# Moving side work between the steps of a fused FNet and gated-FFN kernel

## The chip, the cores and the metric

The kernel runs on one core of one Trainium2 chip. A core has five engines that run side by side, each through its own list of instructions in order: TensorE (PE, matmuls; PEld is its weight load), VectorE (DVE), ScalarE (ACT), GpSimd (POOL) and SyncE (SP, which here only issues DMAs). They wait for each other through semaphores. The metric is the device time of one execution in microseconds, from the first to the last instruction; less is better.

## The reference

The input x has shape (8, 3008, 256), all in float32. A Fourier transform along the sequence and one along the features is taken, and the real part kept. The 8 x 3008 = 24064 rows then pass through a gated feed-forward block.

```python
def _attn_ref(x):
    X = np.fft.fft(x, axis=1)
    X = np.fft.fft(X, axis=2)
    return X.real.astype(np.float32)

def _moe_ref(x, w_gate, w_val, w_out):      # (24064,256) (256,1536) (256,1536) (1536,256)
    gate = 1.0 / (1.0 + np.exp(-(x @ w_gate)))
    val = x @ w_val
    return (gate * val @ w_out).astype(np.float32)
```

## The kernel before

The kernel uses the symmetry of the transform. For a batch, x is loaded as `x4` (128 partitions, 4 mirrored quarters, 6, 256), and *folds* on GpSimd add and subtract the quarters and the mirrored features in place. The sequence transform is then four groups of matmuls (`ev`, `od`) of the folded x with a table `st` of cosines and sines. Each group is *evacuated*: ScalarE copies `ev` out of PSUM, and two sums on VectorE write it into a tile `pk` or `qk` (a third one, `ek`, comes for batches 1 to 7 from `x8`, one feature column of all of x, through `e_fold` and `e_sums`). The feature transform is merged into the weights once, at the start (`G1`, `G2`).

The body is a loop of steps. A batch has 6 chunks of up to 256 columns and 6 pairs of hidden blocks for each, 2 steps a pair: 12 steps a chunk, 72 a batch, 576 in all. While a batch is computed, the next one is folded and transformed in the side jobs of these steps.

```python
def front(p, fh):                    # step: the two matmul pairs, then VectorE
    ...
    for g in range(2):
        mm(pa[:, g], G1[:, g, fs], pk[:, ks], g == 0, True)
    for g in range(2):
        mm(pb[:, g], G2[:, g, fs], qk[:, ks], g == 0, True)
    ae = app.tile(...)
    for g in range(2):
        nc.vector.scalar_tensor_tensor(out=ae[:, g], in0=ek[:, ks], scalar=ge[:, g, f : f + 1],
                                       in1=pa[:, g], op0=ALU.mult, op1=ALU.add)
    z = zp.tile(...)
    nc.vector.tensor_tensor(z[:, :, 0], ae, pb, op=ALU.add)
    nc.vector.tensor_tensor(z[:, :, 1, ::-1], ae, pb, op=ALU.subtract)

def gate(p, fh, z):                  # one step later; h holds the products, sf sums of them
    ...
    nc.vector.tensor_tensor(h[:, fh], z[:, 0], z[:, 1], op=ALU.mult)
    if fh == 0:
        tt(s[:, 2], h[:, 0, 0], h[:, 0, 1], op=ALU.subtract)      # tt is on GpSimd
    else:
        tt(s[:, 0], h[:, 0, 1], h[:, 1, 1], op=ALU.add)
        tt(s[:, 1], s[:, 0], h[:, 0, 0], op=ALU.subtract)
        tt(s[:, 3], h[:, 1, 0], s[:, 1], op=ALU.subtract)

def back(p, part):                   # two pairs later: 3 or 4 products of h or sf with wf, into po
    ...
    if part == 0 and i == NPR - 1:   # copies of po by ScalarE; after the last part: finish
        ...

def finish(b, c, last):              # after a chunk: one job a step from `later`
    ...
    for j in (0, 2, 1):
        nc.scalar.copy(t[:, 2 * j : 2 * j + 2, 0:n], PO[j][:, :, 0:n])
    later.extend([
        lambda: tt(v[:, 0:2], v[:, 6:7].to_broadcast([P, 2, n]), v[:, 0:2], op=ALU.add),
        ...                          # five adds on GpSimd (tile c), then
        lambda: flip(0, 0, 0),       # four transposes on VectorE, and the stores of the output
        ...

fresh = None
for i in range(2 * len(pairs)):
    done, fresh = fresh, front(i // 2, i % 2)
    if done is not None:
        gate(*done)
    if i >= 4:
        back(i // 2 - 2, i % 2)
    ...
    nc.scalar.activation(z[:, 0], z[:, 0], AF.Sigmoid)
    if later:
        later.pop(0)()
    for f in side.pop(i, []):        # side jobs: folds, groups of the transform, loads
        f()
```

A chunk ends in step 3 of the next one, so its five adds fall in steps 3 to 7 of a chunk and its transposes in steps 8 to 11. `side` is filled with `at(i, job)`; `split(i, f)` puts the matmuls and ScalarE's copy in step i and VectorE's sums in step i + 1:

```python
i0 = 2 * NPR                         # 12
at(i0 + 1, e_load, lambda: load_x(1))
for b in range(B - 1):
    s0 = b * per                     # 72 b
    if b:
        at(s0 + 1, lambda b=b: load_x(b + 1))
        if b < B - 2:
            at(s0 + 20, lambda b=b: mirror_x(b + 2))
    f0, g0, gs = (s0 + 9, s0 + 36, 8) if b else (i0 + 9, i0 + 36, 7)
    def folds(f0=f0, b=b):
        for j, f in enumerate(fold_ops(b + 1, 2)):     # 24 jobs
            at(f0 + j, f)
    at(f0 - 1, folds)
    at(g0 - 3, lambda b=b: seq_start(b + 1))
    for j in range(4):
        split(g0 + gs * j, whole, b + 1, j // 2, j % 2)
at(i0 + 14, e_fold)
split(i0 + 18, e_sums)
at(i0 + 20, table_again)
at(8, lambda: mirror_x(1))
at(i0 + 3, mirror_tables, lambda: mirror_x(2))
```

`mirror_x(b)` makes a copy of x in DRAM (`xr`) with the mirrored rows in order, by 9 DMAs; `mirror_tables` does the same for the table (`tr`), which `table_again` loads in place of the first one. All of these are issued by SyncE, as are the stores of the output.

Of the kernel before, what the change touches and what calls it, by code (L numbers as in the profile page):

```python
# [44 lines left out]
NQ = 6  # L45
NP = 126
HP = 64
# [4 lines left out]
def kernel(  # L52
# [10 lines left out]
    nc = tc.nc  # L63
    B, _, _, _, D = xf.shape
# [3 lines left out]
    M = S // 2  # L68
    NK = M + 1
    NE = (M // 2) // 2 + 1  # L70
    NO = (M // 2) // 2
# [4 lines left out]
    HD = D // 2  # L76
    TB = 32
    N3 = NQ // 2
# [31 lines left out]
    def load_x(b):  # L110
        X[b] = xp.tile([P, 4, NQ, D], F32, name="x4", tag="x4")
        for h in range(0, 4, 2):
            if b:
                nc.sync.dma_start(out=X[b][:, h : h + 2], in_=XR[b][:, h : h + 2])
            else:
                nc.sync.dma_start(out=X[b][0:NP, h : h + 2], in_=xf[b, :, h : h + 2])

    def mirrored(dst, src, full):

        for par in range(2):  # L120
            lo = par * HP
            nc.sync.dma_start(out=dst[lo : lo + HP, :, 0:N3], in_=src[0:HP, :, par:NQ:2])
            for q in range(N3):
                t = M // 2 - 2 * q - par
                p0, n = t // NQ, HP - 2 * ((par, q) == (0, N3 - 1))
                nc.sync.dma_start(
                    out=dst[lo : lo + n, :, N3 + q, full:].rearrange("p h d -> h p d"),
                    in_=src[p0 - n + 1 : p0 + 1, :, t % NQ, full:].rearrange("p h d -> h p d")[:, ::-1])

    XR = {}  # L130

    def mirror_x(b):
        XR[b] = dram.tile([P, 4, NQ, D], F32, name=f"xr{b}")
        mirrored(XR[b], xf[b], 0)

        nc.sync.dma_start(out=XR[b][HP - 2 : HP, :, NQ - 1],
                          in_=zero[:, :, 0:D].to_broadcast([2, 4, D]))

    dt = const.tile([P, 2, D], F32, name="dt")
    ST = [const.tile([P, 2, NQ, NE + NO], F32, name="st", tag="st")]  # L140
# [5 lines left out]
    x8 = const.tile([NP, B - 1, 4, NQ], F32, name="x8")  # L146
    zero = const.tile([2, 1, NO], F32, name="zero")
    tr = dram.tile([P, 2, NQ, NE + NO], F32, name="tr")
# [4 lines left out]
            nc.sync.dma_start(out=ST[0][0:NP, t, q : q + nq], in_=stab[:, t, q : q + nq])  # L153

    def mirror_tables():
        mirrored(tr, stab, NE)
        nc.sync.dma_start(out=tr[HP - 2 : HP, :, NQ - 1, NE:],
                          in_=zero.to_broadcast([2, 2, NO]))

    def table_again():  # L160

# [72 lines left out]
    def weight_use(j, other=None):  # L234
        w, c = jobs[j]
        if w == 2:
            forms(WS.pop(j), c)
        else:
            merge(WS.pop(j), w, c, other)
# [14 lines left out]
    def forms(ws, c):  # L254

        w = ws.rearrange("p f (a h j) -> p f h a j", h=2, j=TB)
        f = wf[:, c].rearrange("p m (a j) -> p m a j", j=TB)
        sub = lambda o, a, b: nc.gpsimd.tensor_tensor(o, a, b, op=ALU.subtract)
        nc.scalar.copy(f[:, 0:2], w[:, :, 0])
        nc.scalar.copy(f[:, 2], w[:, 1, 1])  # L260
        sub(f[:, 4], w[:, 0, 1], w[:, 0, 0])
        sub(f[:, 6], w[:, 1, 1], w[:, 0, 1])
        sub(f[:, 5], w[:, 1, 1], f[:, 4])
        sub(f[:, 3], w[:, 1, 0], f[:, 5])
# [4 lines left out]
    def fold_ops(b, nq):  # L269
        x4 = X.pop(b)  # L270
        if not b:
            x4 = x4[0:NP]
        ops = []

        def point(e, i, j, q):
            e.tensor_tensor(x4[:, i, q, 1:D], x4[:, i, q, 1:D], x4[:, j, q, D - 1 : 0 : -1],
                            op=ALU.add)

        def first(e, i, j, q):
            e.tensor_tensor(x4[:, i, q, 0], x4[:, i, q, 0], x4[:, j, q, 0], op=ALU.add)  # L280

        def feat(e, v, r, q):
            e.memset(r[:, q, 0:1], 0.0)
            e.tensor_tensor(r[:, q, 1:HD], v[:, q, 1:HD], v[:, q, D - 1 : HD : -1],  # L284
                            op=ALU.subtract)
            e.tensor_tensor(v[:, q, 1:HD], v[:, q, 1:HD], v[:, q, D - 1 : HD : -1], op=ALU.add)  # L286

        def across(e, blk, q):
            e.tensor_tensor(x4[:, 1 - blk, q], x4[:, 0, q], x4[:, 2, q],  # L289
                            op=(ALU.add, ALU.subtract)[blk])  # L290

        parts = [(x4[:, 1], x4[:, 3]), (x4[:, 0], x4[:, 2])]
        qs = [slice(q, q + nq) for q in range(0, NQ, nq)]
        pool = nc.gpsimd
        if b:

            for i in (0, 2):
                ops += [lambda i=i, q=q: point(pool, i, i + 1, q) for q in qs]
                ops.append(lambda i=i: first(pool, i, i + 1, slice(0, NQ)))
            for blk in range(2):  # L300
                ops += [lambda blk=blk, q=q: across(pool, blk, q) for q in qs]
            for i, op in enumerate((ALU.add, ALU.subtract)):
                for ds in (slice(0, HD), slice(HD, D)):
                    ops.append(lambda i=i, op=op, ds=ds: pool.tensor_tensor(
                        x4[:, 3, i * N3 : (i + 1) * N3, ds], x4[:, 1, 0:N3, ds],
                        x4[:, 1, N3:, ds], op=op))
            parts[0] = x4[:, 3], x4[:, 1]
            for v, r in parts:
                ops += [lambda v=v, r=r, q=q: feat(pool, v, r, q) for q in qs]
        else:  # L310

            def half1(q):
                point(nc.vector, 2, 3, q)
                first(nc.vector, 2, 3, q)
                for blk in range(2):
                    across(nc.vector, blk, q)
                    feat(nc.vector, *parts[blk], q)

            def half2(q):
                across(nc.vector, 0, q)  # L320
                feat(nc.vector, *parts[0], q)
                across(pool, 1, q)
                feat(pool, *parts[1], q)
            for q in qs:
                point(nc.vector, 0, 1, q)
            first(nc.vector, 0, 1, slice(0, NQ))
            point(pool, 2, 3, qs[1])
            first(pool, 2, 3, qs[1])
            ops += [lambda: half1(qs[0]), lambda: half2(qs[1])]
        for blk, (v, r) in enumerate(parts):  # L330
            W[b, blk] = (v[:, :, 0:HD], r[:, :, 0:HD],
                         v[:, :, HD : HD + 1].to_broadcast([v.shape[0], NQ, P]))
        return ops
# [43 lines left out]
    def seq_start(b):  # L377
        PQE[b] = (pqp.tile([P, NK], F32, name="pk", tag="pk"),
                  pqp.tile([P, NK], F32, name="qk", tag="qk"),
                  pqp.tile([P, NK], F32, name="ek", tag="ek"))  # L380
        if b:
            nc.sync.dma_start(out=PQE[b][2], in_=ed[b - 1 : b, :].to_broadcast([P, NK]))
# [2 lines left out]
        return half(lambda q: W[b, blk][what][:, q, :], PQE[b][what], blk, what == 1, other)  # L385


    def e_load():
        for b in range(1, B):
            nc.sync.dma_start(out=x8[:, b - 1], in_=xf[b, :, :, :, HD : HD + 1])  # L390

    def e_fold():
        tt = nc.gpsimd.tensor_tensor
# [32 lines left out]
    pairs = [(b, c, i) for b in range(B) for c in range(len(chunks)) for i in range(NPR)]  # L426
# [162 lines left out]
    for i, f in enumerate(fold_ops(0, NQ // 2)):  # L589
        f()  # L590
        for sums, _, _ in cos:
            sums(*range(i * NQ // 2, (i + 1) * NQ // 2))
# [14 lines left out]
    def at(i, *fs):  # L607
        side.setdefault(i, []).extend(fs)

    def split(i, f, *args):  # L610

        at(i, lambda: at(i + 1, f(*args)))
# [9 lines left out]
    for j in range(3, len(jobs)):  # L622
        w, c = jobs[j]
        at(2 * c + (-3, -2, 1)[w], lambda j=j: weight_use(j))
    i0 = 2 * NPR
    at(i0 + 1, e_load, lambda: load_x(1))

    for b in range(B - 1):
        s0 = b * per
        if b:  # L630
            at(s0 + 1, lambda b=b: load_x(b + 1))
            if b < B - 2:
                at(s0 + 20, lambda b=b: mirror_x(b + 2))
        f0, g0, gs = (s0 + 9, s0 + 36, 8) if b else (i0 + 9, i0 + 36, 7)

        def folds(f0=f0, b=b):
            for j, f in enumerate(fold_ops(b + 1, 2)):
                at(f0 + j, f)
        at(f0 - 1, folds)
        at(g0 - 3, lambda b=b: seq_start(b + 1))  # L640
        for j in range(4):
            split(g0 + gs * j, whole, b + 1, j // 2, j % 2)
    at(i0 + 14, e_fold)
    split(i0 + 18, e_sums)
    at(i0 + 20, table_again)
    at(8, lambda: mirror_x(1))
    at(i0 + 3, mirror_tables, lambda: mirror_x(2))

    fresh = None
    for i in range(2 * len(pairs)):  # L650
# [71 lines left out]
```

## Time and profile before

| | |
|---|---|
| median of 3 runs | 2024.16 us (2021.05 to 2027.18) |
| profiled execution, span | 2017.1 us |
| granted TensorE clock, mean | 0.997 |
| folds of x on GpSimd, 24 jobs a batch (batches 1 to 7) | 1.44 us (points), 1.36 us (across), 1.03 us, 0.93 + 0.86 us (features) for one instruction |
| adds after a chunk on GpSimd (tile c) | 1.56, 1.31, 0.98, 0.72, 0.72 us |
| sums of `h` on GpSimd (tile sf), 4 a pair | 0.74 to 0.77 us each |
| evacuation of a group | 0.47 us on ScalarE, 2 x 0.54 us on VectorE |
| all DMA traffic | 100.32 MB, mean 50 GB/s |

In a row of the profile L100 is the line of the matmul helper, so groups are told apart by their tiles: `po<-sf` is a matmul that reads `sf` and writes `po`. A fp32 matmul shows as two instructions. Behind an arrow in brackets stands how long an engine sat idle before an instruction, and what released it. In a table of waits the columns are the total in us, the number of waits, and the longest.

### The profile page before, as it was taken

To read this page: it belongs to the slowest core of one execution; us is meant where nothing else is said; L and a number is where in the kernel's file an instruction comes from. 1 tells how busy PE (TensorE), PEld (TensorE's weight loads), DVE (VectorE), ACT (ScalarE), POOL (GpSimd) and SP (SyncE) were. 2 spreads that over 40 slices of the span, in tenths; PEclk is the share of its full clock that TensorE was granted. 3 is DMA by queue.
4 is the path that set the end of the run, shared out by engine and by line. 5 is a ranking of instruction groups with operands and counts; after the bars stand their busy time and mean duration, and the time that the engine had idled before them with its cause. 6 is when DMAs were issued, how large, how long until landed. Compare 5 with 4: busy or idle time off the path is not lost.

```text
span 2017.1 us, 28127 instructions
## 1 busy us (share of the span) xinstructions
PE 1977.4 (98%) x9504; PEld 1729.7 (86%) x9504; DVE 1753.4 (87%) x3221; ACT 499.1 (25%) x876; POOL 1361.6 (68%) x1704
## 2 busy tenths in 40 slices
PE   6999999999999999999999999999999999999998
PEld 4888788888988889888898888988889888898888
DVE  7999888988899888998889987998879987898887
ACT  3422222222222222222222222222222222222221
POOL 3778755985569755796558954689546885555655
PEclk9999999999999999999999999999999999999999
DMA  7363302200022001210022100221002010000001
GB/s 274 90 141 114 103 11 78 93 12 11 16 96 70 11 12 37 103 43 14 17 75 72 32 17 11 74 75 35 12 11 74 19 28 12 11 16 16 11 16 25
DMA packets 160814, 100.32 MB, mean 50 GB/s; under 512 B 128419, under 2 KB 151715, under 8 KB 157994
## 3 DMA queue, kind: packets, MB, share of 16 engines
q1 hardware_dynamic: 158850, 98.00, 16.6%
q8 instruction: 76, 1.25, 0.3%
q10 hardware_dynamic: 1822, 0.54, 0.1%
q14 instruction: 66, 0.54, 0.1%
HBM read 73.74 MB, written 50.17 MB: 61 GB/s over the span
## 4 chain that ended last, share of the span: by engine, by line
PE 68%; POOL 20%; DVE 8%; DMA 2%; issue 2%; ACT 0%; DVEq 0%; POOLq 0%; SPq 0%; ACTq 0%
PE po L100 29%; PE pa L100 17%; PE pb L100 16%; PE ev L100 4%; POOL sf L464 3%; POOL sf L461 2%; POOL sf L463 2%; POOL x L289 2%; POOL sf L465 2%; DVE h L459 2%; DVE ae L444 2%; POOL x L286 2%; DVE z L448 1%; POOL x L284 1%; DVE z L447 1%
## 5 line engine op out<-in xcount | busy, mean ns | idle before, releaser
L659 ACT ACTIVATE z<-z 128x512 f32<-128x512 f32 (+1 forms) x576 | 358.5, 622 | 1274.8 <-DVE z L448 1274.7
L444 DVE SCALAR_TENSOR_TENSOR ae<-ek,ge,pa 128x256 f32<-128x256 f32 (+1 forms) x1152 | 490.0, 466 | 182.3 <-PE pa L100 177.9
L100 PE MATMUL pb<-qk,G 128*128 128x256 f32 (+1 forms) x2304 | 582.2, 375 | 3.3 <-DVE ae L444 2.5
L100 PE MATMUL pa<-pk,G 128*128 128x256 f32 (+1 forms) x2304 | 584.6, 376 | 0.0
L100 PE MATMUL po<-sf,wf 128*128 128x256 f32 (+1 forms) x2304 | 537.8, 376 | 12.5 <-POOL sf L464 11.2
L100 PEld LDWEIGHTS po<-sf,wf 128*128 128x128 f32 x2304 | 435.9, 190 | 68.7 <-POOL sf L464 14.4
L100 PEld LDWEIGHTS pa<-pk,G 128*128 128x128 f32 x2304 | 435.2, 190 | 60.2 <-issue 11.3
L100 PEld LDWEIGHTS pb<-qk,G 128*128 128x128 f32 x2304 | 436.9, 190 | 55.8 <-DVE ae L444 4.0
L463 POOL TENSOR_TENSOR sf<-h 128x256 f32<-128x256 f32 (+1 forms) x288 | 213.7, 742 | 364.7 <-DVE h L459 364.7
L459 DVE TENSOR_TENSOR h<-z 128x512 f32<-128x512 f32 (+1 forms) x576 | 447.7, 777 | 0.0
L447 DVE TENSOR_TENSOR z<-ae,pb 128x512 f32<-128x512 f32 (+1 forms) x576 | 390.1, 677 | 61.7 <-DVE ae L444 2.3
L100 PE MATMUL po<-h,wf 128*128 128x256 f32 (+1 forms) x1728 | 412.5, 375 | 0.0
L448 DVE TENSOR_TENSOR z<-ae,pb 128x512 f32<-128x512 f32 (+1 forms) x576 | 386.3, 671 | 0.0
L100 PEld LDWEIGHTS po<-h,wf 128*128 128x128 f32 x1728 | 328.3, 190 | 37.1
L461 POOL TENSOR_TENSOR sf<-h 128x256 f32<-128x256 f32 (+1 forms) x288 | 222.1, 771 | 190.5 <-DVE h L459 185.7
L464 POOL TENSOR_TENSOR sf<-sf,h 128x256 f32<-128x256 f32 (+1 forms) x288 | 215.2, 747 | 22.6
L465 POOL TENSOR_TENSOR sf<-h,sf 128x256 f32<-128x256 f32 (+1 forms) x288 | 214.3, 744 | 22.6
L100 PE MATMUL ev<-st,x 63*128 63x376 f32 (+4 forms) x372 | 103.5, 421 | 7.6 <-DVE x L286 6.9
L100 PE MATMUL od<-st,x 63*128 63x376 f32 (+4 forms) x372 | 102.4, 418 | 0.0
L100 PEld LDWEIGHTS ev<-st,x 63*128 63x128 f32 (+1 forms) x372 | 65.1, 188 | 39.7 <-issue 10.4
L546 ACT COPY c<-po 128x512 f32<-128x512 f32 (+1 forms) x141 | 76.8, 581 | 63.1 <-PE po L100 63.1
L506 DVE STREAM_TRANSPOSE os<-c 128x256 f32<-128x256 f32 x192 | 83.9, 437 | 0.2
(91 smaller groups left out, 806.9 us busy)
## 6 DMA issues: line engine op xcount, KB each, us to landing
x<-xr SPq DMA_DIRECT2D x14, 1536.0 KB
out_dram<-os SPq DMA_DIRECT2D x288, 64.0 KB
xr<-in_xf_dram SPq DMA_DIRECT2D x14, 768.0 KB
xr<-in_xf_dram SPq DMA_DIRECT2D x35, 256.0 KB
ek<-ed SPq DMA_DIRECT2D x7, 752.5 KB
out_dram<-os SPq DMA_DIRECT2D x92, 56.0 KB
x<-in_xf_dram SPq DMA_DIRECT2D x2, 1512.0 KB
tr<-in_stab_dram SPq DMA_DIRECT2D x2, 1129.5 KB
```

The costliest lines, as they stand in the source:

```text
L100: nc.tensor.matmul(o, l, r, start=start, stop=stop, skip_group_check=True)
L444: nc.vector.scalar_tensor_tensor(out=ae[:, g], in0=ek[:, ks], scalar=ge[:, g, f : f + 1], in1=pa[:, g], op0=ALU.mult, op1=ALU.add)
L447: nc.vector.tensor_tensor(z[:, :, 0], ae, pb, op=ALU.add)
L448: nc.vector.tensor_tensor(z[:, :, 1, ::-1], ae, pb, op=ALU.subtract)
L459: nc.vector.tensor_tensor(h[:, fh], z[:, 0], z[:, 1], op=ALU.mult)
L461: tt(s[:, 2], h[:, 0, 0], h[:, 0, 1], op=ALU.subtract)
L463: tt(s[:, 0], h[:, 0, 1], h[:, 1, 1], op=ALU.add)
L464: tt(s[:, 1], s[:, 0], h[:, 0, 0], op=ALU.subtract)
L465: tt(s[:, 3], h[:, 1, 0], s[:, 1], op=ALU.subtract)
L506: nc.vector.transpose(os_[:, s, 0:nb, h, :], t[:, slot, 0 : nb * TB])
L546: nc.scalar.copy(t[:, 2 * j : 2 * j + 2, 0:n], PO[j][:, :, 0:n])
L659: nc.scalar.activation(z[:, 0], z[:, 0], AF.Sigmoid)
```

## The change

Each chunk of 12 steps is divided: steps 3 to 7, in which GpSimd has the five adds of the chunk before, are kept free of folds (`quiet` yields the other seven), and the groups of the transform stand in step 3 (for the first batch in steps 3 and 6). Two smaller parts: x is loaded 6 steps earlier (from step 72 b + 1 to 72 b - 5), and the DMAs that copy from DRAM to DRAM become a list of which one is put in each step (`calm` yields steps 3 to 7). As folds now come earlier or later than before, the feature folds of the part that only the last two groups needed are done first, and those groups come first.

```diff
@@ fold_ops, batches 1 to 7
             for blk in range(2):
                 ops += [lambda blk=blk, q=q: across(pool, blk, q) for q in qs]
+            ops += [lambda q=q: feat(pool, *parts[1], q) for q in qs]
             for i, op in enumerate((ALU.add, ALU.subtract)):
                 ...
             parts[0] = x4[:, 3], x4[:, 1]
-            for v, r in parts:
-                ops += [lambda v=v, r=r, q=q: feat(pool, v, r, q) for q in qs]
+            ops += [lambda q=q: feat(pool, *parts[0], q) for q in qs]
@@ the copies in DRAM: `mirrored` returns 9 single jobs (the zero row first) instead of issuing all
@@ e_load
-    def e_load():
-        for b in range(1, B):
-            nc.sync.dma_start(out=x8[:, b - 1], in_=xf[b, :, :, :, HD : HD + 1])
+    def e_load(b):
+        nc.sync.dma_start(out=x8[:, b - 1], in_=xf[b, :, :, :, HD : HD + 1])
@@ the side jobs
     i0 = 2 * NPR
-    at(i0 + 1, e_load, lambda: load_x(1))
+    quiet = lambda lo: (i for i in range(lo, 2 * len(pairs)) if not 3 <= i % i0 <= 7)
+    calm = lambda lo: (i for i in range(lo, 2 * len(pairs)) if 3 <= i % i0 <= 7)
+    for i, f in enumerate(mirror_x(1)):
+        at(i0 - 3 + i // 2, f)
+    at(i0 + 2, lambda: load_x(1))
+    for b in range(1, B):
+        at(i0 + 2 + b, lambda b=b: e_load(b))
+    for i, f in zip(range(i0 + 3, 2 * i0), mirror_tables()):
+        at(i, f)
+    at(2 * i0 + 3, e_fold)
+    split(2 * i0 + 5, e_sums)
+    at(2 * i0 + 8, table_again)
 
     for b in range(B - 1):
         s0 = b * per
         if b:
-            at(s0 + 1, lambda b=b: load_x(b + 1))
-            if b < B - 2:
-                at(s0 + 20, lambda b=b: mirror_x(b + 2))
-        f0, g0, gs = (s0 + 9, s0 + 36, 8) if b else (i0 + 9, i0 + 36, 7)
-
-        def folds(f0=f0, b=b):
-            for j, f in enumerate(fold_ops(b + 1, 2)):
-                at(f0 + j, f)
-        at(f0 - 1, folds)
-        at(g0 - 3, lambda b=b: seq_start(b + 1))
-        for j in range(4):
-            split(g0 + gs * j, whole, b + 1, j // 2, j % 2)
-    at(i0 + 14, e_fold)
-    split(i0 + 18, e_sums)
-    at(i0 + 20, table_again)
-    at(8, lambda: mirror_x(1))
-    at(i0 + 3, mirror_tables, lambda: mirror_x(2))
+            at(s0 - 5, lambda b=b: load_x(b + 1))
+
+        def folds(f0=s0 - 1 if b else i0 + 8, b=b):
+            for i, f in zip(quiet(f0), fold_ops(b + 1, 2)):
+                at(i, f)
+        at(s0 - 2 if b else i0 + 7, folds)
+        groups = [s0 + i0 * k + 3 for k in (2, 3, 4, 5)] if b else [
+            i0 * k + d for k in (4, 5) for d in (3, 6)]
+        at(groups[0] - 2, lambda b=b: seq_start(b + 1))
+        for j, g in enumerate(groups):
+            split(g, whole, b + 1, 1 - j // 2, j % 2)
+        if b < B - 2:
+            for i, f in zip(calm(s0 + 2 * i0 + 9), mirror_x(b + 2)):
+                at(i, f)
```

In a batch after the first, with steps counted from its start, the folds thus stand in step -1, 0 to 2, 8 to 14, 20 to 26 and 32 to 37 (before: 9 to 32), and the groups in steps 27, 39, 51 and 63 (before: 36, 44, 52 and 60).

More of the change, by code (lines that the diff above doesn't have):

```diff
@@ L118, in mirrored, with rows, mirror @@
     def mirrored(dst, src, full):
-        for par in range(2):
[L121 to L128, printed above, removed]
+        copy = nc.sync.dma_start
+        h, n = dst.shape[1], dst.shape[3] - full
+        ops = [lambda: copy(out=dst[HP - 2 : HP, :, NQ - 1, full:],
+                            in_=zero[:, :, 0:n].to_broadcast([2, h, n]))]
+        def rows(par):
+            copy(out=dst[par * HP : (par + 1) * HP, :, 0:N3], in_=src[0:HP, :, par:NQ:2])
+        def mirror(par, q):
+            t = M // 2 - 2 * q - par
+            lo, p0, n = par * HP, t // NQ, HP - 2 * ((par, q) == (0, N3 - 1))
+            copy(out=dst[lo : lo + n, :, N3 + q, full:].rearrange("p h d -> h p d"),
+                 in_=src[p0 - n + 1 : p0 + 1, :, t % NQ, full:].rearrange("p h d -> h p d")[:, ::-1])
+        for par in range(2):
+            ops.append(lambda par=par: rows(par))
+            ops += [lambda par=par, q=q: mirror(par, q) for q in range(N3)]
+        return ops
     XR = {}
@@ L133, in mirror_x @@
         XR[b] = dram.tile([P, 4, NQ, D], F32, name=f"xr{b}")
-        mirrored(XR[b], xf[b], 0)
-        nc.sync.dma_start(out=XR[b][HP - 2 : HP, :, NQ - 1],
-                          in_=zero[:, :, 0:D].to_broadcast([2, 4, D]))
+        return mirrored(XR[b], xf[b], 0)
     dt = const.tile([P, 2, D], F32, name="dt")
@@ L155, in mirror_tables @@
     def mirror_tables():
-        mirrored(tr, stab, NE)
-        nc.sync.dma_start(out=tr[HP - 2 : HP, :, NQ - 1, NE:],
-                          in_=zero.to_broadcast([2, 2, NO]))
+        return mirrored(tr, stab, NE)
     def table_again():
```

## The prediction

> **What bounds the kernel now.** I read the page first, then the waits of all engines, then TensorE's and GpSimd's instructions in order of time around the waits that end at TensorE. The page's engine line, and its chain of work that ended last:
>
> ```profile
> PE 1977.4 (98%) x9504; PEld 1729.7 (86%) x9504; DVE 1753.4 (87%) x3221; ACT 499.1 (25%) x876; POOL 1361.6 (68%) x1704
> PE 68%; POOL 20%; DVE 8%; DMA 2%; issue 2%; ACT 0%; DVEq 0%; POOLq 0%; SPq 0%; ACTq 0%
> ```
>
> TensorE looks full. The 20% for GpSimd in the chain are not 20% to win: the chain prefers the producer even where its result came just in time. What TensorE lost is in the waits (total us, times, longest):
>
> ```profile
> PEld po L100 <- POOL sf L464: 14.4, 8, 1.9
> PE po L100 <- POOL sf L464: 11.2, 8, 1.5
> PEld po L100 <- POOL sf L465: 6.0, 15, 1.0
> PE pb L100 <- DVE ae L444: 2.5, 3, 1.4
> ```
>
> Eight waits for `sf`, one in each of batches 1 to 6 and two in batch 0. TensorE's order of time in batch 1 shows what one costs (start, length, then what ran):
>
> ```profile
> 411.86 1.03 PE L100 MATMUL pa<-pk,G 128*128 128x256 f32 x4
> ...
> 415.31 1.03 PE L100 MATMUL pa<-pk,G 128*128 128x256 f32 x4
> ...
> 424.86 1.03 PE L100 MATMUL pa<-pk,G 128*128 128x256 f32 x4
> ...
> 428.25 2.37 PE L100 MATMUL po<-sf,wf 128*128 128x256 f32 x8 [1.50 <-POOL sf L464]
> 430.45 1.03 PE L100 MATMUL pa<-pk,G 128*128 128x256 f32 x4
> ```
>
> Each `pa` starts a step. A step with eight `po` instructions lasts 415.31 - 411.86 = 3.45 us; the one at step 35 of the batch lasts 430.45 - 424.86 = 5.59 us. So one wait costs 2.14 us, more than the 1.50 the trace calls idle, because the end of a matmul is modelled. Twelve undisturbed steps take 6 x (3.45 + 3.02) = 38.8 us, the same in every chunk of batch 7, which has no folds: the rest of the time TensorE runs at its own pace. GpSimd in the same moments:
>
> ```profile
> 420.34 1.27 POOL L551 TENSOR_TENSOR c<-c 128x512 f32<-128x512 f32 x1
> ...
> 421.61 0.72 POOL L284 TENSOR_TENSOR x<-x 128x254 f32<-128x254 f32 x1
> ...
> 422.41 1.07 POOL L286 TENSOR_TENSOR x<-x 128x254 f32<-128x254 f32 x1
> ...
> 424.13 0.72 POOL L552 TENSOR_TENSOR c<-c 128x256 f32<-128x256 f32 x1
> ...
> 425.65 1.05 POOL L286 TENSOR_TENSOR x<-x 128x254 f32<-128x254 f32 x1
> ...
> 427.47 0.72 POOL L464 TENSOR_TENSOR sf<-sf,h 128x256 f32<-128x256 f32 x1
> ```
>
> It never rests: adds of the chunk that ended (`c`), folds of the next batch (`x`) and `sf` take turns, and the `sf` that TensorE waits for ends at 428.19.
>
> [...] 98% busy, and yet steps of 5.59 beside 3.45; I use starts of `pa`, not busy time. [...] The only such VectorE instruction of a step is `h`; its mean in 40 us with folds, and in 40 us without:
>
> ```profile
> L459 DVE TENSOR_TENSOR h<-z 128x512 f32<-128x512 f32 x12 | 11.6, 966 | 0.0
> ...
> L459 DVE TENSOR_TENSOR h<-z 128x512 f32<-128x512 f32 x12 | 8.2, 685 | 0.0
> ```
>
> [...] 0.28 us a step dearer, and GpSimd operations of 0.72 us that take 1.07 to 1.18. [...] a load behind others comes late:
>
> ```profile
> 113.21 17.06 SPq L390 DMA_DIRECT2D x<-in_xf_dram  x7
> 130.88 2.20 SPq L114 DMA_DIRECT2D x<-xr  x2
> ...
> 149.54 12.37 SPq L126 DMA_DIRECT2D tr<-in_stab_dram  x3
> ```
>
> and GpSimd's first fold of batch 1 sits 4.00 us idle before 138.96, waiting for that `x`.
>
> **The change, part by part.** No instruction is added or removed; all is a matter of place.
>
> *Folds out of steps 3 to 7 of a chunk.* GpSimd's work in two steps: four `sf` of 0.73, about 0.8 apart, 3.0 us; two folds of 1.27, or feature folds of 0.1 + 0.72 + 0.72, with 0.4 for each lost turn, 2.9 to 3.8; two of the five `c` adds (1.56 + 1.31 + 0.98 + 0.72 + 0.72 = 5.3 in five steps), 2.1. Before, in steps 27 to 31: 3.0 + 3.8 + 2.1 = 8.9 us in a pair of steps of 6.47, so 2.4 us of arrears a pair, about 6 in five steps. After: 3.0 + 2.1 = 5.1 there (1.4 a pair won back), 5.9 to 6.8 elsewhere, about even. The arrears of step 35 should not build up. Removed: 5.59 - 3.45 plus a trifle of 0.05 two steps earlier, 2.19 us in each of six batches = 13.1 us. In batch 0 the steps begin at 211.54, 216.82, 219.85, 225.44: 5.28 - 3.45 = 1.83 and 5.59 - 3.45 = 2.14, together 4.0 us.
>
> *Evacuations at step 3.* A group costs TensorE the same wherever it stands: at step 36, 435.78 - 430.45 = 5.33 against 3.02, and 0.1 in the next step. VectorE's two sums of 0.54 now fall where it has no transposes (0.44 each), TensorE's 2.4 or 4.1 us of group let VectorE catch up, and ScalarE's copies of `po` are done within the group. But I see no wait of TensorE there before: 0 us won.
>
> *x sooner.* Batch 0 loses GpSimd's 4.00 us idle, but TensorE did not wait then: 0. In later batches the load goes out 6 steps earlier, the fold starts 10 earlier; about 4 steps (13 us) plus the lag of GpSimd remain, and the load took about 10 us (two slices of the DMA view after its issue at 316.4). Hidden.
>
> *Copies one a step.* SyncE does not follow the steps; it runs ahead until an instruction of its own queue waits. The copies wait for nothing but older copies, so they still go out in bunches, now two of five and four between the output's stores. 0 us. Around the table they do matter. The seven loads of `x8` used to go first; now they alternate with the copies of the table and stand behind `x`. Until the last `x8`: `x` 10.1, seven loads of 2.2 = 15.4, two row copies of 3.2 = 6.4, three mirrors of 4.2 = 12.6, sum 44.5 us [...]. From the mirrored x's landing, about 116, that is 160.5. The fold of `x8` was at 154.3 before and would be reached at about 154 to 157 now; TensorE reaches the sums of it at step 29, 155.4 + 3.45 = 158.9. With 1.1 us for the fold TensorE may wait 161.6 - 158.9 = 2.7 us, and GpSimd loses some 5. I count +3 us, once.
>
> *VectorE in batch 0.* After the sums, two operations on `er` of 1.5 and 1.6 us put VectorE back; steps 34 to 38 lose 2.1 us altogether. With folds out of steps 27 to 31, half may go: -1.
>
> *A shorter lead.* The fold of the features that group one needs ends its last slice in step 25; the group stands in step 27, the distance was 4 steps before. GpSimd's folds ran 1.5 to 3 steps behind their place in steps 9 to 25 of the profile; the matmuls of the last slice stand two thirds into the group. Nearly tight: +0.4 us in six batches, about +2.5.
>
> Sum: -13.1 - 4.0 - 1 + 3 + 2.5 = -12.6, rounded to -13 with other trifles. 2024.2 - 13 is 2011; I lean one further down, 2010, as the two risks are taken at more than their likeliest size.
>
> **The rivals.** (a) *All arrears go and no risk comes true*: -18, 2006. For it: GpSimd was the only cause of the eight large waits; even before, folds in all of steps 9 to 25 with the `c` adds in five of them caused no wait. (b) *The wait moves*: the group at step 27 waits for features, or `sf` now comes late at steps 14 or 26, some 2 us a batch as before: 2020 to 2026. Against it: slack of about three steps, and loads even with the pace. (c) *VectorE becomes the bound*: its step is 2 x 0.47 + 0.69 + 0.68 + 0.69 = 3.0, with folds 3.3, with a transpose 3.7, against 3.24; folds now share steps 8 to 11 with the transposes, four times 0.45 us of arrears. Against it: the profile had that in steps 20 to 23 too, without a wait, since four banks of `pa` and `pb` hold a step. It would make +0.5 us in some chunks, up to 2020. (d) *The table's copies stall batch 0* longer, 8 to 10 us once: 2016.
>
> **Range and chances.** The lower end is (a) with a few us of spread (single times lie between 2021 and 2027): 2001. The upper end is (d), or a good part of (b): 2019. Two per cent are 40 us; TensorE's losses found above are 13.1 + 4.0 + 2.1 = 19, so faster by 2% is all but excluded, and slower by 2% would need 3 us lost in each chunk: 0.01 and 0.02.
>
> **What would show it.** Right: waits of `po` for `sf` near 0, every step 35 at 3.45 us; groups still adding about 2.4 and 4.2 us; GpSimd's total busy time about as before, `h` too. Wrong: `ev` waiting for a fold of `x` at step 27; `pe` waiting for the fold of `x8` by more than 5 us; waits of `pb` for VectorE in most batches; or `x` landing after its first fold's turn in batches 2 to 7.

## The result and the profile after

The changed kernel takes 2009.95 us (median of 4 runs, 2009.52 to 2012.41) against 2024.94 us before: ratio 0.9931, 95% interval 0.9913 to 0.9948, 0.7% faster. Forecast: 2010.0, between 2001 and 2019. Close as that is, two terms of its sum were well off and in opposite directions, and a part of the gain was not in the sum at all.

The page of the changed kernel, its engine line and the chain that ended last:

```profile
PE 1975.4 (98%) x9504; PEld 1738.0 (87%) x9504; DVE 1767.0 (88%) x3221; ACT 498.3 (25%) x876; POOL 1332.2 (66%) x1704
PE 92%; DMA 3%; SPq 3%; DVE 1%; issue 0%; ACT 0%; POOL 0%; ACTq 0%; DVEq 0%; POOLq 0%
```

Busy shares have hardly moved, but GpSimd's 20% of the chain are gone; SyncE's queue has 3%, new, and DMAs 3% instead of 2%. TensorE's longest waits now (total us, times, longest):

```profile
PEld pa L100 <- issue: 11.9, 29, 1.3
PEld ps L100 <- POOL ws L236: 9.1, 1, 9.1
PEld pe L100 <- POOL x L399: 7.2, 1, 7.2
```

The lines of `po` waiting for L464 and L465 of before, 14.4 and 6.0 us, have no successor here worth naming (0.3 us on the page). `pe` waiting for the fold of `x8` (L399) is new. TensorE's order of time around step 35, here in batch 3:

```profile
913.31 1.03 PE L100 MATMUL pa<-pk,G 128*128 128x256 f32 x4
...
916.34 1.03 PE L100 MATMUL pa<-pk,G 128*128 128x256 f32 x4
917.20 1.03 PE L100 MATMUL pb<-qk,G 128*128 128x256 f32 x4
918.06 1.89 PE L100 MATMUL po<-sf,wf 128*128 128x256 f32 x8
919.79 1.03 PE L100 MATMUL pa<-pk,G 128*128 128x256 f32 x4
```

Step 35 lasts 919.79 - 916.34 = 3.45 us, where before it was 5.59. Undisturbed steps take 3.02 and 3.45 us in turn; this is called the pace below. And step 29 of batch 0, in the same view:

```profile
155.86 1.03 PE L100 MATMUL pa<-pk,G 128*128 128x256 f32 x4
156.73 1.03 PE L100 MATMUL pb<-qk,G 128*128 128x256 f32 x4
157.59 1.89 PE L100 MATMUL po<-sf,wf 128*128 128x256 f32 x8
166.31 4.17 PE L100 MATMUL pe<-st,x 126*7 126x377 f32 x24 [6.83 <-POOL x L399]
170.42 1.77 PE L100 MATMUL pa<-pk,G 128*128 128x256 f32 x4
```

What it waits for is the fold of `x8` on GpSimd, and that waits for a DMA:

```profile
165.41 0.27 POOL L397 TENSOR_TENSOR x<-x 126x42 f32<-126x42 f32 x1 [6.84 <-DMA x<-in_xf_dram]
```

TensorE sits idle for 6.83 us, and then its next matmuls are slow: `pe` takes 4.17 us, the first `pa` 1.77 instead of 1.03. In the kernel before the same 24 instructions took 2.09 us:

```profile
162.00 2.09 PE L100 MATMUL pe<-st,x 126*7 126x377 f32 x24
```

The granted clock in stretches of time gives the reason. Behind a stretch and its length stand the busy us of PE, PEld, DVE, ACT and POOL with their instructions, then the clock, the DMA share and GB/s (the stretches: before, during and after the wait, and later):

```profile
150.00:158.00 8.00, 8.00 (x38) 7.06 (x38) 7.79 (x13) 3.03 (x6) 7.21 (x9) 1.00 0.32 31
158.00:166.00 8.00, 1.48 (x7) 0.95 (x5) 3.79 (x6) 1.04 (x2) 1.08 (x4) 0.72 0.88 165
166.00:172.00 6.00, 5.69 (x28) 2.72 (x29) 0.00 (x0) 0.93 (x2) 4.68 (x8) 0.52 0.24 68
172.00:180.00 8.00, 8.00 (x38) 7.04 (x37) 6.62 (x13) 1.10 (x2) 3.92 (x4) 1.00 0.18 51
```

In the 6 us after the wait the mean clock is 0.52. By stages, from the starts of the first `pa` of each batch in the two traces:

| | before, us | after, us |
|---|---|---|
| start, to the first step | 48.7 | 49.1 |
| batch 0 | 263.7 | 267.3 |
| batches 1 to 6 together | 1463.2 | 1450.0 |
| batch 7 and the end | 241.5 | 241.5 |
| span | 2017.1 | 2008.0 |

So the change wins 13.2 us in six batches and loses 3.6 in batch 0. The traces differ by 9.1 us, the medians of the times by 15.0; the sixth run below shows where the rest lies.

### The profile page after: what moved, and what is told of

Same layout as the page of the kernel before. It is cut to its first block, busy times and chain, and to the rows that moved or that the text cites. A ratio compares the mean times of both kernels' runs of the same rounds, so it can differ in the third digit from the quotient of the medians.

```text
span 2008.0 us, 28130 instructions
## 1 busy us (share of the span) xinstructions
PE 1975.4 (98%) x9504; PEld 1738.0 (87%) x9504; DVE 1767.0 (88%) x3221; ACT 498.3 (25%) x876; POOL 1332.2 (66%) x1704
## 4 chain that ended last, share of the span: by engine, by line
PE 92%; DMA 3%; SPq 3%; DVE 1%; issue 0%; ACT 0%; POOL 0%; ACTq 0%; DVEq 0%; POOLq 0%
PE po L100 41%; PE pa L100 23%; PE pb L100 23%; PE ev L100 4%; SPq L132 1%; DMA ge<-G 1%; DMA st<-in_stab_dram 1%; SPq L127 1%; DMA xr<-in_xf_dram 1%; SPq L123 0%; PE ps L100 0%; DMA x<-in_xf_dram 0%; PE od L100 0%; SPq L393 0%; DMA raw<-in_moe_w_gate_dram 0%
## 5 line engine op out<-in xcount | busy, mean ns | idle before, releaser
L466 POOL TENSOR_TENSOR sf<-h 128x256 f32<-128x256 f32 (+1 forms) x288 | 206.9, 718 | 443.4 <-DVE h L462 443.4
L100 PEld LDWEIGHTS pb<-qk,G 128*128 128x128 f32 x2304 | 438.3, 190 | 52.7 <-DVE ae L447 4.1
L462 DVE TENSOR_TENSOR h<-z 128x512 f32<-128x512 f32 (+1 forms) x576 | 471.4, 818 | 0.0
L464 POOL TENSOR_TENSOR sf<-h 128x256 f32<-128x256 f32 (+1 forms) x288 | 206.4, 717 | 128.8 <-DVE h L462 118.5
L467 POOL TENSOR_TENSOR sf<-sf,h 128x256 f32<-128x256 f32 (+1 forms) x288 | 207.2, 719 | 22.6
```

What stands on the lines that cost most here:

```text
L100: nc.tensor.matmul(o, l, r, start=start, stop=stop, skip_group_check=True)
```

## The experiments

All were profiled and timed in three or five rounds beside the kernel before, whose own times in these comparisons run from 2020.4 to 2033.7 us. "By stages" is read as in the table above.

**1. The loads of x8 ahead of the table's copies.**

```diff
     at(i0 + 2, lambda: load_x(1))
     for b in range(1, B):
-        at(i0 + 2 + b, lambda b=b: e_load(b))
+        at(i0 + 2, lambda b=b: e_load(b))
```

> The changed kernel with the seven loads of x8 issued right after the load of x, ahead of the copies of the table, instead of alternating with them. Theory A (the last x8 load is late because it queues behind three table mirrors and two row copies, some 19 us of copies): the fold of x8 finds its data, TensorE's wait for it of 6.8 us and the slow clock after it (some 2 us) go; step 29 falls from 14.55 us to 5.5 or 6, the span by 8.5 to 9 us, to about 1999. Rival B (the fold of x8 stands only two steps ahead of its sums, GpSimd is late there whatever the DMAs do): GpSimd does the fold at once but TensorE still waits 4 us or more; span 2003 to 2006.

Measured: 2001.84 us (2001.66 to 2003.47), ratio to before 0.9876 (0.9857 to 0.9896), span 1999.9. SyncE's queue of the changed kernel, in order of time:

```profile
120.74 0.94 SPq L393 DMA_DIRECT2D x<-in_xf_dram  x1
122.15 7.85 SPq L123 DMA_DIRECT2D tr<-zero  x1
...
145.48 0.84 SPq L393 DMA_DIRECT2D x<-in_xf_dram  x1
146.37 5.38 SPq L132 DMA_DIRECT2D tr<-in_stab_dram  x1
151.80 0.84 SPq L393 DMA_DIRECT2D x<-in_xf_dram  x1
152.68 5.42 SPq L127 DMA_DIRECT2D tr<-in_stab_dram  x1
158.14 0.83 SPq L393 DMA_DIRECT2D x<-in_xf_dram  x1
```

and of this run:

```profile
120.75 0.82 SPq L114 DMA_DIRECT2D x<-xr  x2
121.62 20.32 SPq L393 DMA_DIRECT2D x<-in_xf_dram  x7
141.98 1.72 SPq L123 DMA_DIRECT2D tr<-zero  x1
```

The last x8 load goes out before 142 instead of at 158.14, as no copy of the table stands between the loads. Batch 0 takes 258.3 us instead of 267.3. Theory A holds. Of rival B a little is left: TensorE still waits 0.41 us.

```profile
160.73 2.31 PE L100 MATMUL pe<-st,x 126*7 126x377 f32 x24 [0.41 <-POOL x L399]
```

**2. The fold and the sums of x8 later.**

```diff
-    at(2 * i0 + 3, e_fold)
-    split(2 * i0 + 5, e_sums)
-    at(2 * i0 + 8, table_again)
+    at(2 * i0 + 11, e_fold)
+    split(2 * i0 + 13, e_sums)
+    at(2 * i0 + 16, table_again)
```

> The changed kernel with the fold of x8, its sums and the reload of the table 8 steps later (steps 35, 37 and 40 instead of 27, 29 and 32); no DMA changes its place ahead of them. Theory A (the wait is for the last x8 load, which lands at about 165 us) gives the fold at 185 us all its data: wait gone, span down by 8 to 9 us. Rival B (distance of two steps) keeps a wait of some us. Rival C (VectorE's two slow sums of er, now in the steps with folds and near the transposes, put TensorE back as in the kernel before) gives back 2 us of it: span 2001 rather than 1999.

Measured: 2002.56 us (2002.14 to 2003.44), ratio 0.9879 (0.9859 to 0.9898). Batch 0 takes 257.8 us; the span of 2001.7 has a start that is 3.2 us longer than the changed kernel's (52.3 us), which no edit touched. The wait is gone with no DMA moved ahead of it, so it was one for data, and `pe` takes 2.09 us again. Rival C gave back 0.3 us (one step of 3.35 instead of 3.02), not 2.

**3. Before, with its folds five steps sooner.**

```diff
-            at(s0 + 1, lambda b=b: load_x(b + 1))
+            at(s0 - 5, lambda b=b: load_x(b + 1))
...
-        f0, g0, gs = (s0 + 9, s0 + 36, 8) if b else (i0 + 9, i0 + 36, 7)
+        f0, g0, gs = (s0 + 4, s0 + 36, 8) if b else (i0 + 9, i0 + 36, 7)
```

> The kernel before with two numbers changed: in batches 1 to 6 x is loaded 6 steps sooner and the 24 folds start in step 4 instead of 9, still in every step, so they end in step 27 and only one feature fold, not five, meets the adds after a chunk; the groups stay where they were. Theory D (feature folds, 1.5 to 1.9 us each, together with the adds make the arrears; the cheaper folds with the adds do not): the six waits at step 35 go, 13 us, span about 2004, with the two waits of batch 0 left. Rival E (any fold in steps 3 to 7 makes arrears that TensorE meets): folds still fill steps 4 to 7 and 15 to 19, the wait moves to another step and the gain is under 5 us.

Measured: 2014.62 us (2013.20 to 2017.16), ratio 0.9938 (0.9921 to 0.9955). Batches 1 to 6 take 1457.5 us: 5.7 of the 13.2 us are won. TensorE in batch 2:

```profile
656.59 1.03 PE L100 MATMUL pa<-pk,G 128*128 128x256 f32 x4
657.46 1.03 PE L100 MATMUL pb<-qk,G 128*128 128x256 f32 x4
659.07 2.37 PE L100 MATMUL po<-sf,wf 128*128 128x256 f32 x8 [0.59 <-POOL sf L464]
661.28 1.03 PE L100 MATMUL pa<-pk,G 128*128 128x256 f32 x4
```

The wait has moved from step 35 to 31 and shrunk: 661.28 - 656.59 = 4.69 us, 1.24 over the pace instead of 2.14. Neither theory's number came: D asked for 13 us, E for under 5.

**4. The changed kernel with folds in every step.**

```diff
-            for i, f in zip(quiet(f0), fold_ops(b + 1, 2)):
+            for i, f in zip(range(f0, 2 * len(pairs)) if b else quiet(f0), fold_ops(b + 1, 2)):
```

> The changed kernel with its folds in every step from -1 to 22 in batches 1 to 6 instead of in the quiet steps alone; all else (x sooner, order of the feature folds, groups in step 3, batch 0) as changed. Theory D: only points, across and the middle folds meet the adds after a chunk, so no wait of TensorE for sf comes back: 2008 to 2009 of span, the same as changed. Rival E (keeping the folds out of steps 3 to 7 is what won the time): waits come back near steps 8 or 20, about 2 us a batch, 13 us in all, span about 2021.

Measured: 2019.18 us (2017.50 to 2021.68), ratio 0.9962 (0.9947 to 0.9977). Batches 1 to 6 take 1458.5 us: 8.5 of the 13.2 us come back, though just two of the folds in steps 3 to 7 and 15 to 19 are not points, sums across or middle folds: a one-row fold and one feature fold. D falls, and E's 13 us are too many. TensorE in step 23 of batch 2:

```profile
633.97 1.03 PE L100 MATMUL pa<-pk,G 128*128 128x256 f32 x4
...
636.12 2.36 PE L100 MATMUL po<-sf,wf 128*128 128x256 f32 x8 [0.26 <-POOL sf L467]
638.32 1.03 PE L100 MATMUL pa<-pk,G 128*128 128x256 f32 x4
```

This step is 638.32 - 633.97 = 4.35 us long, 0.90 over the pace. What fits both runs is a sum over the whole stretch. Four traces show how far GpSimd is behind, as a lag: the end of the `sf` sum that TensorE waited for (L464 before), less the start of the step in which its `h` is made, in steps, in batch 3. It rests at 1.7 to 2.0 in all. In the kernel before it grows, with dips, through all 24 folds to 3.6 (2.1 at step 18, 2.8 at 20, 2.4 at 26, 3.3 at 30, 3.6 at 32), in run 3 to 3.5 at step 28, in run 4 to 3.5 at step 20, and in the changed kernel never over 2.5. TensorE asks for that `sf` three steps after, behind `pa` and `pb`, at about 3.5. So the lag of a run without pauses reaches the limit whether feature folds meet the adds or stand beside them; the pauses pay it back. That sooner folds alone won 43% fits a smaller pile at the worst place, but how the 43% come about was not tried further.

**5. The groups at their old places.**

```diff
-        groups = [s0 + i0 * k + 3 for k in (2, 3, 4, 5)] if b else [
+        groups = [s0 + k for k in (36, 44, 52, 60)] if b else [
```

> The changed kernel with the groups of batches 1 to 6 back at steps 36, 44, 52 and 60; folds in the quiet steps, x sooner, batch 0 as changed. Theory F (the place of a group costs nothing, the folds' places won it all): groups cost 2.3 and 4.1 us again plus 0.1 in the next step, no wait for sf, span 2008 within 1 us. Rival G (the evacuations have to stand in the steps after a chunk, or VectorE's sums collide with its transposes at steps 44 and 45): waits of TensorE for VectorE of 0.5 us or more at two groups a batch, span 2012 or more.

Measured: 2012.85 us (2011.83 to 2013.67), ratio 0.9926 (0.9912 to 0.9941), span 2010.3. Batches 1 to 6 take 1450.0 us, each 241.67, the same as changed to 0.01 us. The start, which no edit touched, took 51.9 us against 49.1, and batch 0 was 0.5 us shorter; that is the whole difference in span. F holds: the evacuations' new place is worth nothing.

**6. The loads of x8 last, and the kernel before again.**

```diff
-    for b in range(1, B):
-        at(i0 + 2 + b, lambda b=b: e_load(b))
     for i, f in zip(range(i0 + 3, 2 * i0), mirror_tables()):
         at(i, f)
+    for b in range(1, B):
+        at(2 * i0, lambda b=b: e_load(b))
```

> The changed kernel with the seven loads of x8 issued in step 24, behind all copies of the table and the stores of a chunk. Theory A (loads of x8 land when their queue is done with what stands ahead): three mirrors of 4.2 us and some stores more stand ahead of the last load, so TensorE's wait grows from 6.8 to about 18 to 20 us and the slow clock after it stays about 2 us; span about 2020. Under a rival in which the x8 loads themselves are what takes long, the wait stays near 7 us and the span near 2008.

Measured: 2026.68 us (2023.99 to 2030.87), ratio 1.0000 (0.9991 to 1.0008), as slow as the kernel before. The span of 2025.0 us is 17.0 above the changed kernel's: 13.4 in batch 0 by the place of seven small loads, and 3.6 in the start (52.7 us), which no edit touched. TensorE waits 20.2 us, at the upper end of what theory A had.

```profile
183.15 4.18 PE L100 MATMUL pe<-st,x 126*7 126x377 f32 x24 [20.20 <-POOL x L399]
187.25 1.95 PE L100 MATMUL pa<-pk,G 128*128 128x256 f32 x4
```

`pe` is as slow after 20.2 us of idling (4.18) as after 6.83 (4.17). Then the kernel before, unchanged:

> The kernel before once more, for its spread: its times lie between 2020 and 2032 us while each changed version stays within 4 us, and the profile taken before lies at the low end. Theory H (the arrears of GpSimd sit at the edge of what TensorE feels, so small shifts make some waits longer or add some): a profile of a longer execution shows more than 8 waits for sf, or longer ones, and nothing else longer. Rival I (the start, up to the first step at 48.7 us, or the end is what varies): the first step or the last stores shift by as many us.

Measured: 2027.13 us (2020.58 to 2030.26), ratio to itself 1.0004 (0.9990 to 1.0018); this profile has a span of 2028.5. Steps 34 to 37 of batches 1 to 3 in its stretches of time, with the clock before the DMA share:

```profile
426.40:443.90 17.50, 15.89 (x86) 13.12 (x85) 12.98 (x25) 3.04 (x6) 14.80 (x21) 1.00 0.14 31
670.30:689.40 19.10, 17.50 (x85) 14.25 (x84) 12.81 (x25) 3.00 (x5) 14.34 (x21) 0.91 0.14 29
915.80:935.00 19.20, 17.58 (x85) 14.27 (x84) 12.90 (x25) 3.02 (x6) 14.40 (x21) 0.91 0.13 28
```

The first is as in the earlier profile, where all six read 17.50 us at a clock of 1.00. In batches 2 to 5 of this execution the same four steps take 19.1 to 19.2 us at 0.91. TensorE's rows there, in batch 2:

```profile
676.66 3.43 PE L100 MATMUL po<-sf,wf 128*128 128x256 f32 x8 [1.50 <-POOL sf L464]
679.89 1.69 PE L100 MATMUL pa<-pk,G 128*128 128x256 f32 x4
```

and the clock of the same moments in shorter stretches:

```profile
672.00:675.00 3.00, 3.00 (x15) 2.45 (x13) 2.90 (x7) 0.63 (x1) 2.92 (x5) 1.00 0.42 87
675.00:676.60 1.60, 0.17 (x1) 0.00 (x0) 1.50 (x4) 0.00 (x0) 1.52 (x3) 1.00 0.00 0
676.60:678.00 1.40, 1.23 (x4) 0.81 (x5) 1.40 (x3) 0.63 (x1) 1.32 (x4) 0.93 0.00 0
678.00:680.00 2.00, 2.00 (x6) 1.55 (x6) 0.31 (x1) 0.00 (x0) 1.92 (x4) 0.50 0.27 58
```

The wait is the same 1.50 us, and the table of waits has the very line of the earlier profile:

```profile
PEld po L100 <- POOL sf L464: 14.4, 8, 1.9
```

H falls: neither more nor longer waits. What varies is whether the clock dips after a wait: 1.7 us in each of four batches, 1470.0 - 1463.2 = 6.8 us. Rival I is right for another part: the start is 52.9 us against 48.7. Together 10.9 of the 11.4 us between the two profiles.

**7. The best of these: x8 first, and its sums two steps later.**

```diff
     at(i0 + 2, lambda: load_x(1))
     for b in range(1, B):
-        at(i0 + 2 + b, lambda b=b: e_load(b))
+        at(i0 + 2, lambda b=b: e_load(b))
...
-    split(2 * i0 + 5, e_sums)
+    split(2 * i0 + 7, e_sums)
```

> The changed kernel with the x8 loads right after the load of x and the sums of x8 in step 31 instead of 29. The rest of rival B (0.7 us of step 29 left in the run with the loads first, as the fold is done 0.4 us after TensorE is ready) should go: span about 1999, 2001.2 us of time. If VectorE's slow sums of er now meet its transposes and folds (step 32), 1 to 2 us come back in steps 34 to 38 and nothing is won.

Measured: 2001.73 us (2001.14 to 2005.57), ratio 0.9878 (0.9860 to 0.9897), span 1999.4. Batch 0 takes 257.6 us, 0.7 less than in run 1, as expected; the times of the two cannot be told apart. Both are about 8 us faster than the changed kernel, and no step of 34 to 38 is over its pace.

## Why the prediction was right, and where not

| term of the sum | predicted, us | measured in the traces, us |
|---|---|---|
| six waits at step 35 | -13.1 | -13.2 |
| two waits in batch 0 | -4.0 | -4.0 |
| VectorE in batch 0 | -1 | -2.1 |
| sums of x8 | +3 | +9.6 |
| shorter lead of the features | +2.5 | 0 |
| start, which was not in the sum | 0 | +0.4 |

*Folds out of steps 3 to 7*: right in mechanism and size. In the profile before (batch 3) the lag, taken in us, is 5.5 at rest, 7.5 at step 26 and 12.9 at step 32, so those steps add 5.4, where I had estimated about 6. Runs 3 and 4 refine it: I had put the arrears of step 35 down to the five steps 27 to 31 alone and called the rest about even; the lag grows in the rest as well, which fits that run 4 brings 8.5 us back with only one feature fold among those it puts into steps 3 to 7 and 15 to 19.

*Evacuations*, 0: right, by run 5. *x sooner*, 0 by itself: no wait of TensorE came from it in any run.

*Copies one a step*: that SyncE would run ahead was right (in batch 1 the first five copies, placed in steps 111 to 115 from 445.95 us on, went out from 440.65 to 446.52), and my estimate of 44.5 us of queue was nearly so: from the issue of x at 119.88 to GpSimd's fold at 165.41 are 45.5. The mis-sized term is what I made of it, a wait of 2.7 us counted as 3. The mirrored x was complete later than the 116 I had assumed (x was issued only at 119.88), so TensorE waited 6.83; and I had no slow clock in the sum: 4.17 - 2.09 = 2.1 us in `pe` and 0.6 in the next step. In all 9.6 us, which is rival (d), that I had set apart from the sum.

*VectorE in batch 0*: put at half its size; steps 34 to 38 are at their pace, in run 7 too, where the sums of x8 stand only one step later than in the kernel before. *Shorter lead*: the order was as I read it and the distance nearly as small, but the last slice was not late. GpSimd in batch 3, and TensorE's first instruction of the group:

```profile
887.95 0.10 POOL L287 MEMSET x<- 128x2 f32 x1
888.01 0.73 POOL L288 TENSOR_TENSOR x<-x 128x254 f32<-128x254 f32 x1
888.81 1.05 POOL L290 TENSOR_TENSOR x<-x 128x254 f32<-128x254 f32 x1
...
889.79 0.58 PE L100 MATMUL ev<-st,x 63*128 63x376 f32 x1
```

The slice ends at 889.86; the group's first matmul starts at 889.79, and those that read this slice some 2.6 us later. I had charged 0.4 us a batch for a margin that was there.

One sign failed without harm: the mean of `h` on VectorE is 818 ns after against 777 before, not about the same. And two remarks were off that no term rests on: 2% slower would have been some 54 us more than forecast, 1.1 us in each of 48 chunks and not 3; and in batch 7 the chunks take 38.8 us except for the first (38.1) and the narrower last.

The sum of the measured column is -9.3, near the -9.1 between the spans. The medians differ by 15.0: the profile before is of an execution without dips of the clock in its batches, at the low end of its times; run 6 shows one with them. The mean clock of each execution, which is on record, says the same of the others. In the 49 executions of the kernel before that the comparisons hold, it lies between 0.991 and 0.997, and the time falls by 2.05 us for each 0.001 (correlation -0.91); a dip as in run 6 takes 3.41 x 0.5 / 2025 = 0.0008 off the mean and costs 1.7 us. The 13 executions of runs 1, 2 and 7, which have none of the large waits, all stand at 0.996 or 0.997. So most of the spread is time at half clock, and it goes with the waits; how much of it lies in the batches and how much in the start is seen in one execution only.

So the forecast of 2010 met the time with errors that balanced, which is luck: 6.6 us too little for the sums of x8, 3.6 too much for VectorE and the lead, and some 6 us of gain that the one profile of the kernel before did not show.

## What to carry to other kernels

Measure an in-order helper engine by how far it lags behind its place, over the whole stretch: here it cost nothing until the lag reached the distance to its reader (about 3.5 steps), and pauses brought it back to 2.5 with no work removed. Ask what stands ahead of a small load in its DMA queue: here the last load of x8, behind copies of the table, went out at 158.14 us and kept TensorE waiting for 6.83; issued ahead of them (run 1) or used later (run 2) it won 9.0 and 9.5 us in batch 0. Add to each wait of TensorE what its clock may lose after it: here 2.7 us after 6.83 idle, and 0 or 1.7 after 1.50.

## What was not expected of the hardware

The clock of TensorE after its waits. After 6.83 and after 20.2 us of idling `pe` took 4.17 and 4.18 us for 2.09. In the changed kernel the clock read 0.50 from 161.50 to 171.74 us, 10.24 us that begin within the wait; in run 6, in the kernel before, it read 0.50 between 678 and 680 us. The trace's clock records there have four dips to 0.5 within the batches, of 3.4 us each, from 677.8, 923.6, 1169.3 and 1415.1 us.

What I had not expected is how short a wait suffices. A wait that shows as 1.50 us idle, and costs 2.14 us of pace, brought a dip in four of six batches of one execution and in none of six of another, with the same instructions and the same waits.

The traces show in what the four differ. Within a trace all changes of the clock lie whole multiples of 3.413 us from one another, to within about 0.001 of one, so they give a grid: in the changed kernel they come at 18.143, 24.970, 161.503 and 171.743 us, 2, 40 and 3 such intervals apart. Take the place where a wait of 1.50 us begins, as a share of the interval of this grid that it falls in. In the four waits with a dip it is 0.23, 0.16, 0.10 and 0.04; in the eleven such waits without one (the profile before, run 6 and run 3, batch 0 included) it lies between 0.33 and 1.00. A batch with a dip lasts 245.55 us or 71.94 intervals, so the next wait began 0.06 earlier in its interval, and the dips came in four batches in a row; without one it lasts 243.86 us or 71.44 intervals. So in these traces every such wait up to 0.23 had a dip and none from 0.33 on. No run put a wait at a chosen place, so this is seen in fifteen waits and not tried, and what makes the grid was not shown.

The start of the program varied from 48.7 to 52.9 us between executions, in instructions that no edit touched. The four traces with 10.24 us of half clock in it begin their steps at 50.7 to 52.9 us, the six with 6.83 at 48.7 to 51.9; the cause was not tried.
